# Four tiles of a second MoE moved into the first MoE's last block, and 22 of its 24 tiles transposed by VectorE and DMA

## Chip, cores, metric

One core of a Trainium2 chip. The metric is device time in microseconds (us), median of the runs; the profile is of one execution of the same program.

## What is computed

A linear attention over 4 sequences of 768 steps gives 3072 tokens of 384 features. Two MoE layers follow. Cut to what matters:

```python
# attention, per head: state = w_t * state + k_t v_t^T ;  y_t = r_t (state + u k_t v_t^T)
x = attn_out.transpose(0, 2, 1, 3).reshape(3072, 384)
# first MoE, d_ff = 1536
x = (silu(x @ w_gate) * (x @ w_val)) @ w_out
# second MoE, d_ff = 1024
h = x @ w_in
e = exp(h - max(h))
solu = h * e / (sum(e) + 1e-9)
ln = (solu - mean(solu)) / sqrt(var(solu) + 1e-6) * g_ln
out = ln @ w_out2
```

Every fp32 matrix product is done as three products of a high part and a low part (`xh`, `xl`, and weights split the same way).

## The kernel before

**Planner.** Nothing is issued in program order. Each step is put into a `Graph` with an engine, an assumed duration, a priority (a due time in us), and the keys that it reads and writes. `emit` (line 134) runs a list schedule over these numbers, and the order that comes out is the order on each engine's queue. Each queue then runs in order, so an instruction that waits holds everything behind it. All DMAs are issued from SyncE (SP).

**First MoE.** Tokens come in six blocks of 512 (`q` = 0 to 5). `moe1_unit` (line 744) does one of the 12 slices of `d_ff`: two projections of 9 matmuls of 128x512 into a PSUM bank each (`proj`, gate and value), SiLU on ScalarE (ACT, line 768), the product on VectorE (DVE, line 773), its split into `mh` on ACT and `ml` on DVE (line 776), then 9 matmuls with `w_out` into banks 3 to 5 (`o_part`). At a block's end three copies move the result to SBUF and three DMAs spill it to DRAM (`x2d`). The attention of block q+1 runs inside block q; the last block has none.

**Second MoE.** 24 tiles of 128 tokens, `tile2` (line 982). Weights are staged by DMA (line 922), decoded on DVE and split (lines 934 to 949), and the spilled tokens are loaded again and split (`load_x2`, line 897). A tile is:

- "H": 18 matmuls of 128x512 into `hp`, two PSUM banks (line 998);
- row maximum on DVE (line 1011), exponential on ACT (line 1013), product with `hp` on DVE (line 1016), statistics on DVE in operations of one column (lines 1019 to 1048), normalization on DVE or ACT (`norm`, line 1050);
- transposition of the 128x1024 result. For 8 tiles TensorE (PE) does it in 8 matmuls against the identity (line 1069), and ACT and DVE split the PSUM result into `th` and `tl`. For the 16 tiles in `PAIRS` DVE transposes 32x32 blocks (line 1085), 16 DMAs for each pair of tiles move the blocks across partitions (line 1092), ACT makes `th` and GpSimd (POOL) `tl` (line 977);
- "O": 24 matmuls of 128x384 (line 1104), a copy on ACT, a DMA to the output.

**Memory.** Pools are released and opened again between the stages by steps without an engine (`CTL`): `to_w2` after the attention, `to_p2` and `to_ps2` after all work of the first MoE. So before the change tile 0 alone can start early (`H0`, line 987, `hw`, line 990); every other tile waits for the second half of `hp` or the buffers of `p2`.

Of the kernel before, what the change touches and what calls it, by code (L numbers as in the profile page):

```python
# [30 lines left out]
NQ = S // (2 * C)  # L31
# [7 lines left out]
NEX = 4  # L39
# [12 lines left out]
H0 = -17.0  # L52
TLD = 0
NORM = {"ACT": 1.15, "DVE": 0.73}
GB, NTH = 2, 4
PAIRS = (5, 8, 10, 12, 14, 16, 18, 20)
# [177 lines left out]
def attn_moe_moe2_kernel(  # L234
# [41 lines left out]
    BK = slots(psp, "ps", [128, 512], 6) + slots(psa, "psa", [128, 512], 2)  # L276
# [17 lines left out]
    WD = {d: [w1p.tile([128, 2, KD, 128], F32R, name=f"{x}{d[0][0]}{d[0][1]}") for x in "hl"] for d in duos}  # L294
# [442 lines left out]
    nmid, nsg, silu, spills = [0], [0], [], []  # L737
# [6 lines left out]
    def moe1_unit(j, m):  # L744
# [41 lines left out]
        def later():  # L786
            for k in range(KD):
                o_part(k)
            if m == M1 - 1:
                for k in range(KD):  # L790
                    late = q < NQ - 1
                    if late:
                        xs, xk = ST[k].bitcast(F32), [("st", k, 0), ("st", k, 1)]
                    else:
                        xs, xk = sg_slot() if q == 0 or k < 2 else (None, "x2s0")
                        xk = [xk]

                    def spill(k=k, xs=xs):
# [3 lines left out]
                              [("bank", 3 + k)], xk)  # L802
# [27 lines left out]

    st0, st1 = att_prep(0), att_prep(1)
# [22 lines left out]
    last_unit, R = pend, {}  # L854

    def release(name):
        pools.pop(name)[0].close()

    def to_w2():
        release("st1")  # L860
        release("att")
        release("psa")
        R["h"] = [open_pool("ps2a", space=PSUM, side="right", reuse_waits="tile").tile([128, F2], F32, name="hp0")]
        p = open_pool("w2", side="right", reuse_waits="tile")
        R["i2h"], R["i2l"] = (p.tile([128, KD, F2], F32R, name=x) for x in ("i2h", "i2l"))
        R["o2h"], R["o2l"] = (p.tile([128, M2, DM], F32R, name=x) for x in ("o2h", "o2l"))
        R["g"] = p.tile([128, M2], F32, name="g_sb")
        raw, n = p.tile([128, 2 * F2], RAW, name="sv"), max(DM * sz, TB)
        R["st"] = [raw[:, i * n:(i + 1) * n] for i in range(2)]
        R["ex"] = [raw[:, 0:F2].bitcast(F32)]  # L870
        R["dc"] = slots(p, "dv", [128, DM], 2, U32)
        R["x2s0"] = p.tile([128, TB], F32, name="x2s0")
        R["sm"] = slots(p, "sm", [128, 16], NEX)
        R["bs"] = slots(p, "bs", [128, 2, 6], NEX)

    def to_ps2():
        release("ps")
        p = open_pool("ps2", space=PSUM, reuse_waits="tile")
        R["h"].append(p.tile([128, F2], F32, name="hp1"))
        R["b"] = slots(p, "pb", [128, 512], 4)  # L880

    def to_p2():
        release("w1")
        p = open_pool("p2", reuse_waits="tile")
        R["x2s"] = slots(p, "x2s", [128, TB], 3)
        R["ex"] += slots(p, "ex", [128, F2], NEX - 1)
        R["th"] = slots(p, "th", [128, M2, 128], NTH, F32R)
        R["tl"] = slots(p, "tl", [128, M2, 128], NTH, F32R)
        R["tb"] = slots(p, "tb", [128, GB, F2], 2)
        R["xt"] = slots(p, "xt", [128, GB, 4, F2 // 4], 2)  # L890
        R["ob"] = slots(p, "ob", [128, DM], 3)
# [3 lines left out]
    g.add("CTL", 0.0, 0.0, to_w2, [], ["w2"], after=st_nodes)  # L895
    g.dma(0.1, T5, lambda: nc.sync.dma_start(out=R["g"], in_=g_ln), ["w2"], ["g"])
    def load_x2(q, prio):
        for k in range(KD):
            xk = "x2s0" if q == 0 else ("x2s", k)

            def x2s(k=k):
                return R["x2s0"] if q == 0 else R["x2s"][k]

            g.dma(0.8, prio, lambda k=k, v=x2s: nc.sync.dma_start(out=v(), in_=x2d[q][:, k]),
                  [("x2d", q, k), "w2" if q == 0 else "p2"], [xk])
            g.add("ACT", t_act(TB), prio, lambda k=k, v=x2s: copy(XH[q % 2][:, k], v())(),
                  [xk], [("xh", q % 2, b) for b in range(B)] + [("x2h", q % 2, k)])
            g.alt({"DVE": t_dve(TB)} if q == 0 else {"POOL": t_pool(TB)}, prio,
                  lambda e, k=k, v=x2s: tt(ENG[e], XL[q % 2][:, k], v(), XH[q % 2][:, k].bitcast(F32), ALU.subtract)(),
                  [xk, ("x2h", q % 2, k)], [("xl", q % 2, b) for b in range(B)] + [("x2l", q % 2, k)], port=True)  # L910

    pieces = [("i", k, c0, cn) for k in range(KD) for c0, cn in ((0, 384), (384, 384), (768, 256))]
    pieces += [("o", m, 0, DM) for m in range(M2)]
    for j, (w, k, c0, cn) in enumerate(pieces):
        pr = T5 + 2.0 * j
        i = j % 2
        if j == XP:
            load_x2(0, pr)
        sk, dk = ("sv", i), ("dv", i)
# [8 lines left out]
        def step(z, i=i, cn=cn, raw=raw):  # L928
            decode_op(z, R["st"][i][:, 0:2 * cn].rearrange("p (n t) -> p n t", t=2), raw())
# [32 lines left out]
    shuffled, late = [n + j for n in PAIRS for j in range(GB)], []  # L962

    def splits2(n, s2, j, pt):
        j3 = n % NTH
        xk = [("xt", s2, a, p) for a in range(4) for p in range(4)]

        def ops(y, hi):
            v = slice(4 * y, 4 * y + 4)
            x = R["xt"][s2][:, j].rearrange("p a (m t) -> p m a t", m=M2)[:, v]  # L970
            h, l = (R[z][j3][:, v].rearrange("p m (a t) -> p m a t", a=4) for z in ("th", "tl"))
            if hi:
                copy(h, x)()
            else:
                return l, x, h.bitcast(F32)

        for y in range(2):
            g.add("ACT", t_act(512), pt + SPL, partial(ops, y, True), xk, [("th", j3, y)])
            g.alt({"POOL": t_pool(512), **({"DVE": t_dve(512)} if TLD else {})}, pt + SPL,
                  lambda e, y=y: tt(ENG[e], *ops(y, False), ALU.subtract)(), xk + [("th", j3, y)], [("tl", j3, y)])  # L980

    def tile2(n):
        q, b = order[n]
        i = n % NEX
        j3 = n % NTH
        jb = n % 3
        p0 = TEND + 8.0 * n + (0 if n else H0)
        s = slice(b * 128, (b + 1) * 128)
        hk = [("hb", n % 2, 0), ("hb", n % 2, 1)]
        hw = "ps2" if n % 2 else "w2"  # L990
        xh_, xl_ = XH[q % 2], XL[q % 2]

        def hp():
            return R["h"][n % 2]

        def h_mm(j):
            f = slice(j * 512, (j + 1) * 512)
# [5 lines left out]
        for j in range(2):  # L1003
            g.add("PE", 2.06, p0 + 2 * j, lambda j=j: h_mm(j),
                  [(x, q % 2, k) for x in ("x2h", "x2l") for k in range(KD)] + i2keys + [hw], [hk[j]])

        def c(x):
            return R["sm"][i][:, x:x + 1]

        pr = p0 + -12.0  # L1010
        g.add("DVE", 1.15, pr, lambda: DVE.tensor_reduce(out=c(0), in_=hp(), axis=AX.X, op=ALU.max, negate=True),
              hk, [("m", i)])
        g.add("ACT", 1.1, pr, lambda: ACT.activation(out=R["ex"][i], in_=hp(), func=AF.Exp, bias=c(0), scale=1.0,
                                                     accum_out=c(2)), hk + [("m", i), "table", "p2" if i else "w2"],
              [("ex", i), ("s", i)] + [("sv", z) for z in range(0 if n else 2)])
# [12 lines left out]
        def ts2(out, in0, s1, s2, op0, op1=None):
            kw = {} if op1 is None else {"op1": op1}
            return lambda: DVE.tensor_scalar(out=c(out), in0=c(in0), scalar1=s1, scalar2=s2, op0=op0, **kw)  # L1030

        def mul3(out, x, y, z):
            return lambda: DVE.scalar_tensor_tensor(out=c(out), in0=c(x), scalar=-1.0 if z == 11 else c(y),
                                                    in1=c(y if z == 11 else z), op0=ALU.mult, op1=ALU.mult)
# [61 lines left out]
        def finish():  # L1096
            if n in shuffled:
                splits2(n, s2, j2, pt)
# [114 lines left out]
```

## Time and profile before

| | us |
|---|---|
| median of 3 runs (755.42 to 755.64) | 755.6 |
| the profiled execution | 756.6 |
| its span in the trace | 754.8 |
| PE busy in the span | 744.7 |
| DVE busy | 568.0 |
| ACT busy | 327.5 |
| POOL busy | 60.7 |

The profiled execution took 1.0 us more than the median, and 1.8 us of it lie outside the span. Matmuls are pipelined, so a row's duration overlaps the next one; what a matmul takes from PE is the distance from its start to the next start. The stages in the trace: attention and first MoE to about 550 us, second MoE from there to the end, with the last block of the first MoE from about 476 us.

### The profile page before, as it was taken

To read this page: it belongs to the slowest core of one execution; us is meant where nothing else is said; L and a number is where in the kernel's file an instruction comes from. 1 tells how busy PE (TensorE), PEld (TensorE's weight loads), DVE (VectorE), ACT (ScalarE), POOL (GpSimd) and SP (SyncE) were. 2 spreads that over 40 slices of the span, in tenths; PEclk is the share of its full clock that TensorE was granted. 3 is DMA by queue.
4 is the path that set the end of the run, shared out by engine and by line. 5 is a ranking of instruction groups with operands and counts; after the bars stand their busy time and mean duration, and the time that the engine had idled before them with its cause. 6 is when DMAs were issued, how large, how long until landed. Compare 5 with 4: busy or idle time off the path is not lost.

```text
span 754.8 us, 16325 instructions
## 1 busy us (share of the span) xinstructions
PE 744.7 (99%) x6512; PEld 647.3 (86%) x6512; DVE 568.0 (75%) x1188; ACT 327.5 (43%) x700; POOL 60.7 (8%) x53
## 2 busy tenths in 40 slices
PE   7999999999999999999999999999999999999998
PEld 7899988899888888888888888888788988889998
DVE  8799999978867777767865552588388899999930
ACT  4898653533334333323433312434245352554531
POOL 0000000000000000000000000000022231622440
PEclk9999999999999999999999999999999999999999
DMA  8986643432423223333332210543041224234321
GB/s 232 283 257 236 187 123 110 122 92 82 127 63 101 80 78 114 105 88 89 95 103 75 61 30 10 164 136 120 0 137 53 67 63 126 73 101 107 100 85 43
DMA packets 58780, 81.52 MB, mean 108 GB/s; under 512 B 18128, under 2 KB 42448, under 8 KB 58704
## 3 DMA queue, kind: packets, MB, share of 16 engines
q1 hardware_dynamic: 58704, 80.48, 36.6%
q8 instruction: 51, 0.84, 0.5%
q14 instruction: 25, 0.20, 0.1%
HBM read 59.47 MB, written 9.44 MB: 91 GB/s over the span
## 4 chain that ended last, share of the span: by engine, by line
PE 80%; DVE 10%; DMA 4%; ACT 3%; issue 2%; SPq 1%; ACTq 0%; DVEq 0%
PE ps L733 14%; PE ps L734 14%; PE ps L735 14%; PE pb L1107 4%; PE pb L1109 4%; PE pb L1108 4%; PE hp L999 4%; PE hp L1000 4%; PE hp L1001 4%; PE psa L733 3%; PE psa L734 3%; PE psa L735 3%; DMA feat<-feat 2%; SPq L1092 1%; PE ps L661 1%
## 5 line engine op out<-in xcount | busy, mean ns | idle before, releaser
L733 PE MATMUL ps<-xh,hg 128*128 128x512 f32 (+1 forms) x339 | 124.2, 366 | 0.0
L735 PE MATMUL ps<-xh,lg 128*128 128x512 f32 (+1 forms) x339 | 122.5, 361 | 0.0
L734 PE MATMUL ps<-xl,hg 128*128 128x512 f32 (+1 forms) x339 | 122.4, 361 | 0.0
L733 PE MATMUL ps<-mh,ho 128*128 128x512 f32 (+1 forms) x252 | 91.5, 363 | 0.0
L734 PE MATMUL ps<-ml,ho 128*128 128x512 f32 (+1 forms) x252 | 90.6, 360 | 0.1
L325 ACT ACTIVATE mh<-sg 128x512 fp32r<-128x512 f32 (+1 forms) x84 | 47.7, 570 | 99.0 <-DVE sg L322 98.5
L735 PE MATMUL ps<-mh,lo 128*128 128x512 f32 (+1 forms) x252 | 90.4, 359 | 0.0
L733 PEld LDWEIGHTS ps<-xh,hg 128*128 128x128 f32 x339 | 64.0, 189 | 10.0
L735 PEld LDWEIGHTS ps<-xh,lg 128*128 128x128 f32 x339 | 64.0, 189 | 10.0
L734 PEld LDWEIGHTS ps<-xl,hg 128*128 128x128 f32 x339 | 64.0, 189 | 9.4
L322 DVE TENSOR_TENSOR sg<-sg,ps 128x512 f32<-128x512 f32 (+1 forms) x62 | 37.1, 599 | 44.4 <-PE ps L735 43.3
L322 DVE TENSOR_TENSOR ml<-sg,mh 128x512 fp32r<-128x512 f32 (+1 forms) x84 | 51.0, 608 | 22.2 <-ACT mh L325 21.9
L322 POOL TENSOR_TENSOR xl<-x2s,xh 128x512 fp32r<-128x512 f32 x15 | 19.6, 1328 | 589.3 <-ACT xh L325 589.3
L1107 PE MATMUL pb<-o2h,th 128*128 128x384 f32 x192 | 64.9, 338 | 0.6 <-ACT ob L325 0.6
L1109 PE MATMUL pb<-o2h,tl 128*128 128x384 f32 x192 | 64.5, 336 | 0.0
L1108 PE MATMUL pb<-o2l,th 128*128 128x384 f32 x192 | 64.5, 336 | 0.0
L768 ACT ACTIVATE sg<-ps 128x512 f32<-128x512 f32 (+1 forms) x51 | 28.0, 549 | 78.2 <-PE ps L735 77.9
L733 PE MATMUL psa<-xh,hg 128*128 128x512 f32 (+1 forms) x165 | 60.1, 364 | 0.0
L735 PE MATMUL psa<-xh,lg 128*128 128x512 f32 (+1 forms) x165 | 58.6, 355 | 0.0
L734 PE MATMUL psa<-xl,hg 128*128 128x512 f32 (+1 forms) x165 | 58.6, 355 | 0.0
L999 PE MATMUL hp<-i2h,xh 128*128 128x512 f32 x144 | 57.0, 396 | 0.5 <-DVE sv L1016 0.5
L1000 PE MATMUL hp<-i2l,xh 128*128 128x512 f32 x144 | 56.6, 393 | 0.0
(173 smaller groups left out, 1679.7 us busy)
## 6 DMA issues: line engine op xcount, KB each, us to landing
tok<-tok SPq DMA_DIRECT2D x20, 576.0 KB, 3.8
feat<-feat SPq DMA_DIRECT2D x24, 448.0 KB, 4.5
xt<-tb SPq DMA_DIRECT2D x128, 64.0 KB, 2.0
feat<-feat SPq DMA_DIRECT2D x24, 231.4 KB, 2.7
vv<-vv SPq DMA_DIRECT2D x24, 192.0 KB, 2.7
st<-w_gate SPq DMA_DIRECT2D x12, 384.0 KB, 4.7
st<-w_val SPq DMA_DIRECT2D x12, 384.0 KB, 5.9
st<-w_out SPq DMA_DIRECT2D x12, 384.0 KB, 5.1
```

Of the source, the lines that this page charges most:

```text
L322: return lambda: eng.tensor_tensor(out=out, in0=in0, in1=in1, op=op)
L325: return lambda: ACT.activation(out=out, in_=in_, func=AF.Copy)
L733: PE.matmul(out=o, lhsT=wh, rhs=xhi, start=first, stop=False, **kw)
L734: PE.matmul(out=o, lhsT=wh, rhs=xlo, start=False, stop=False, **kw)
L735: PE.matmul(out=o, lhsT=wl, rhs=xhi, start=False, stop=last, **kw)
L768: lambda: ACT.activation(out=sg, in_=pg.t[:, 0:n], func=AF.Silu), [pg.key], [sk]))
L999: PE.matmul(out=hp()[:, f], lhsT=xh_[:, k, s], rhs=R["i2h"][:, k, f], start=(k == 0), stop=False)
L1000: PE.matmul(out=hp()[:, f], lhsT=xh_[:, k, s], rhs=R["i2l"][:, k, f], start=False, stop=False)
L1001: PE.matmul(out=hp()[:, f], lhsT=xl_[:, k, s], rhs=R["i2h"][:, k, f], start=False, stop=(k == KD - 1))
L1107: PE.matmul(out=po(), lhsT=th[:, m], rhs=R["o2h"][:, m], start=(m == 0), stop=False)
L1108: PE.matmul(out=po(), lhsT=th[:, m], rhs=R["o2l"][:, m], start=False, stop=False)
L1109: PE.matmul(out=po(), lhsT=tl[:, m], rhs=R["o2h"][:, m], start=False, stop=(m == M2 - 1))
```

## The change

- Tiles 0 to 3 of the second MoE may start inside the first MoE's last block: they need `w2` alone (one `hp`, `H0` = -56), and their exponentials are put between two loads of ScalarE's function tables (`early`), since that block's SiLU needs another table. There are 12 table loads in place of 2.
- Tiles go in pairs, but for 22 and 23. Maximum, exponential, product and moments stay one tile's (`front`); the rest of the statistics is done for both tiles at once in operations of two columns (`stats`, `back`).
- All pairs, so tiles 0 to 21, are transposed by DVE and DMA (`shuffle`); tiles 22 and 23 by PE (`by_pe`).
- `norm` runs on ACT only.
- PSUM and SBUF are cut into more pools, so that a buffer of the second MoE waits only for what lay in its own place (`to_p2(z)`, `to_psg`, `to_pso`); seven buffers `ex` in place of four; five staging places for `w_in`, lying in the `ex` buffers.
- The attention of the last tiles is spread over a shorter time (`MARG` = 16), and block 4's result is spilled through other buffers.

```diff
-NEX = 4
+NEX = 7
-H0 = -17.0
+H0 = -56.0
+PE2 = -9.0
-NORM = {"ACT": 1.15, "DVE": 0.73}
+NORM = {"ACT": 1.24}
-PAIRS = (5, 8, 10, 12, 14, 16, 18, 20)
+NE = 4
+SOLO, NSM = (22, 23), 4
...
-    ADV, ADV2, MARG = 4.0, 12.0, 0.0
+    ADV, ADV2, MARG = 4.0, 12.0, 16.0
...
-        d = (bstart[j + 1] - bstart[j] - (0.0 if n < NYS else MARG)) / (a1 - a0)
+        d = (bstart[j + 1] - bstart[j] - (MARG if n >= NT - B else 0.0)) / (a1 - a0)
...
+    SV = [(2,), (4,), (3,), (0, 1)]
...
-        i = j % 2
+        i, y = j % 2, (0, 1, 4, 3, 2)[j % 5] if w == "i" else j % 2
...
-    g.add("CTL", 0.0, 0.0, to_p2, [], ["p2"], after=[i for i in work if i not in spills])
-    g.add("CTL", 0.0, 0.0, to_ps2, [], ["ps2"], after=work)
+    for z in range(M1 // 2):
+        g.add("CTL", 0.0, 0.0, partial(to_p2, z), ["w2"] + ([("p2", z - 1)] if z else []),
+              [("p2", z)] + [(x, y, m) for x in ("wh", "wl") for y in "gvo" for m in (2 * z, 2 * z + 1)])
+    g.add("CTL", 0.0, 0.0, to_psg, ["w2"], ["psg"], after=gvs)
+    g.add("CTL", 0.0, 0.0, to_pso, ["psg"], ["pso"], after=gvs + spills)
...
+    def tile_p0(n):
+        return TEND + 8.0 * n + (H0 if n < NE else 0)
...
+        def early():
+            ACT.preload_act_table_set("natural_log_exp_and_others")
+            if last is not None:
+                last()
+            soft()
+            ACT.preload_act_table_set("silu_and_others")
...
+    def stats(gi, grp):
...
+        g.add("DVE", 0.25, pr, lambda: two(6, 5, 3)(), kv + [("is", z)], [("v0", z)], port=True)
+        g.add("DVE", 0.25, pr, lambda: two(6, 6, 3)(), [("is", z)], [("v0", z)], port=True)
...
+        def log():
+            ACT.activation(out=c(7), in_=c(6), func=AF.Ln)
+            ACT.activation(out=c(7), in_=c(7), func=AF.Exp, scale=-0.5)
...
+    def back(gi, grp):
...
+            g.alt(NORM, pr, norm, [("nb", z), ("rs", z)], [("ex", i)], port=True)
+        (shuffle if w == GB else by_pe)(gi, grp)
...
+    def shuffle(gi, grp):
+        s2, pt = pairs.index(grp) % 2, tile_p0(grp[-1]) + 10.0
+        for j, n in enumerate(grp):
+            g.add("DVE", 1.24, pt - 22.0, lambda j=j, n=n: DVE.transpose(
...
+        for a in range(4):
+            for p in range(4):
+                g.dma(0.66, pt - 9, lambda a=a, p=p: nc.sync.dma_start(
...
+                g.add("POOL", t_pool(512), pt + SPL, lambda y=y, f=ops: tt(POOL, *f(y, False), ALU.subtract)(),
...
+        g.add("PE", 4.17, TEND + 8.0 * n + 35.0 + (LAG if lag else 0), o_mm,
```

How the instructions move, at three places. **PE, tile 1's way to its O, just behind the first MoE** (`hp` is H's result, `ident,ex` a transposition, `pb` and `pc` O's result). Before:

```order
L1001 MATMUL hp_5949<-i2h,xl_97 128x512
L1069 MATMUL pb_5950<-ident,ex_5926 128x128 x4
L1069 MATMUL pb_5951<-ident,ex_5926 128x128 x4
L999 MATMUL hp_5400<-i2h,xh_96 128x512
L1000 MATMUL hp_5400<-i2l,xh_96 128x512
L1001 MATMUL hp_5400<-i2h,xl_98 128x512
```

After:

```order
L1016 MATMUL hp_6092<-i2h,xh_117 128x512
L1017 MATMUL hp_6092<-i2l,xh_117 128x512
L1018 MATMUL hp_6092<-i2h,xl_119 128x512
L1185 MATMUL pc_6178<-o2h,th_5977 128x384
L1186 MATMUL pc_6178<-o2l,th_5977 128x384
L1187 MATMUL pc_6178<-o2h,tl_6047 128x384
```

The 8 transpositions of the tile are gone; over the whole program PE has 64 before and 16 after, and 48 instructions fewer in all (4964 and 4916), nothing else on PE being added or taken away.

**ACT in the first MoE's last block** (`sg` is the SiLU, `mh` the split of the product, `o2h` the weights of the second MoE, `ex` with `sm` the exponential of a tile). Before, the end of the block:

```order
L768 ACTIVATE sg_100<-ps_80 128x512
L936 ACTIVATE o2h<-dv_5410,g_sb 128x384
L325 ACTIVATE mh_102<-sg_100 128x512
L768 ACTIVATE sg_99<-ps_79 128x512
L325 ACTIVATE mh_101<-sg_99 128x512
L768 ACTIVATE sg_100<-ps_78 128x512
L960 ACT_TABLE_LOAD
L1013 ACTIVATE sv,sm_5413<-hp_5400,sm_5413 128x1024
L325 ACTIVATE mh_102<-sg_100 128x512
```

After, from the block's third slice on:

```order
L329 ACTIVATE mh_122<-sg_120 128x512
L960 ACTIVATE o2h<-dv_5302,g_sb 128x384
L960 ACTIVATE o2h<-dv_5301,g_sb 128x384
L1035 ACT_TABLE_LOAD
L1032 ACTIVATE ex_5298,sm_5304<-hp_5288,sm_5304 128x1024
L1039 ACT_TABLE_LOAD
L772 ACTIVATE sg_121<-ps_100 128x512
L960 ACTIVATE o2h<-dv_5302,g_sb 128x384
L960 ACTIVATE o2h<-dv_5301,g_sb 128x384
L329 ACTIVATE mh_123<-sg_121 128x512
```

Each early tile's exponential stands between two table loads, ahead of the SiLU of a later slice.

**SP, the loads of the second MoE's weights and tokens** (`sv` and `ex` are staging places, `w_in` and `w_out` here the second MoE's weights, `x2d` the spilled tokens). Before:

```order
L922 DMA sv<-w_in 128x768 x2
L904 DMA x2s_5412<-x2d_89 128x512
L922 DMA sv<-w_in 128x512
L922 DMA sv<-w_in 128x768
L904 DMA x2s_5412<-x2d_89 128x512
```

After:

```order
L946 DMA ex_5300<-w_in 128x512
L927 DMA ex_5298<-x2d_110 128x512
L946 DMA sv<-w_out 128x768 x2
L927 DMA ex_5299<-x2d_110 128x512
L332 DMA x2d_114<-sg_121 128x512
L332 DMA x2d_114<-x2s_5303 128x512
L332 DMA x2d_114<-sg_120 128x512
L946 DMA sv<-w_out 128x768 x2
L927 DMA x2s_5303<-x2d_110 128x512
```

The last third of the first 512 tokens is loaded into the buffer through which block 4's last third was just spilled, behind two more weight loads.

## Rows read from the trace of the kernel before

**Rows 1.** The page's first part: busy time and instructions of each engine.
```profile
PE 744.7 (99%) x6512; PEld 647.3 (86%) x6512; DVE 568.0 (75%) x1188; ACT 327.5 (43%) x700; POOL 60.7 (8%) x53
```
**Rows 2.** Windows: stretch, its length, busy time by engine, granted clock, DMA share.
```profile
375.00:450.00 75.00, 75.00 (x698) 61.98 (x697) 44.26 (x89) 24.87 (x53) 0.00 (x0) 1.00 0.23 68
505.00:535.00 30.00, 30.00 (x133) 24.70 (x133) 22.62 (x43) 10.08 (x18) 0.00 (x0) 1.00 0.32 93
535.00:555.00 20.00, 19.50 (x90) 15.85 (x89) 9.40 (x20) 8.65 (x15) 0.00 (x0) 1.00 0.20 67
635.00:720.00 85.00, 85.00 (x431) 77.15 (x430) 80.16 (x171) 43.67 (x90) 34.22 (x27) 1.00 0.38 99
```
**Rows 3.** Chain that ended last, at the first MoE's end: start, length, what.
```profile
542.57 1.28 ACT L960
...
543.86 1.21 ACT sv L1013 x2
...
545.25 1.14 DVE sv L1016
...
546.44 0.50 PE hp L999
```
**Rows 4.** Timeline of PE at its two waits: start, length, instruction, idle time before.
```profile
545.55 0.39 PE L735 MATMUL ps<-mh,lo 128*128 128x512 f32 x1
546.44 0.50 PE L999 MATMUL hp<-i2h,xh 128*128 128x512 f32 x1 [0.50 <-DVE sv L1016]
...
626.12 0.39 PE L1001 MATMUL hp<-i2h,xl 128*128 128x512 f32 x1
627.06 0.45 PE L1107 MATMUL pb<-o2h,th 128*128 128x384 f32 x1 [0.56 <-ACT ob L325]
```
**Rows 5.** Timeline of PE at one tile's transposition.
```profile
568.11 1.03 PE L1069 MATMUL pb<-ident,ex 128*128 128x128 f32 x8
568.90 0.48 PE L999 MATMUL hp<-i2h,xh 128*128 128x512 f32 x1
```
**Rows 6.** Groups by line: count, busy us, mean ns of one, idle before and releaser.
```profile
L322 DVE TENSOR_TENSOR ml<-sg,mh 128x512 fp32r<-128x512 f32 (+1 forms) x84 | 51.0, 608 | 22.2 <-ACT mh L325 21.9
L325 ACT ACTIVATE mh<-sg 128x512 fp32r<-128x512 f32 (+1 forms) x84 | 47.7, 570 | 99.0 <-DVE sg L322 98.5
L322 POOL TENSOR_TENSOR tl<-xt,th 128x512 fp32r<-128x512 f32 x32 | 40.6, 1298 | 81.7 <-ACT th L325 73.6 <-DMA out<-ob 8.1
L322 DVE TENSOR_TENSOR sg<-sg,ps 128x512 f32<-128x512 f32 (+1 forms) x62 | 37.1, 599 | 44.4 <-PE ps L735 43.3 <-ACT sg L768 0.7
...
L1011 DVE TENSOR_REDUCE sm<-hp 128x1 f32<-128x1024 f32 x24 | 29.2, 1216 | 6.0 <-PE hp L1001 5.5
L768 ACT ACTIVATE sg<-ps 128x512 f32<-128x512 f32 (+1 forms) x51 | 28.0, 549 | 78.2 <-PE ps L735 77.9
```
**Rows 7.** Chain, a pair of tiles shuffled: product of the second, first DMA issue, landing.
```profile
597.25 1.13 DVE ex L1016
...
602.11 0.68 SPq L1092
...
611.80 2.00 DMA xt<-tb
```
**Rows 8.** One line's and one tile's instructions: count, ns min/median/max, first and last start.
```profile
L922 SPq DMA_DIRECT2D sv<-w_in x9: 328/328/447, 476.2 to 499.9; - x9
...
L322 DVE TENSOR_TENSOR i2l<-dv,i2h x9: 416/551/559, 483.7 to 505.9; 128x384 fp32r<-128x384 f32 x6, 128x256 fp32r<-128x256 f32 x3
```
**Rows 9.** Timeline of DVE, the last attention tile: sum of its output, split of it.
```profile
449.73 0.62 DVE L322 TENSOR_TENSOR tok<-psa,tok 128x192 f32<-128x192 f32 x2 [0.98 <-PE psa L664]
...
463.62 0.56 DVE L322 TENSOR_TENSOR xl<-tok,xh 128x384 fp32r<-128x384 f32 x1 [1.33 <-ACT xh L325]
```
**Rows 10.** DMA issues: count, KB each, median us from issue to landing.
```profile
x2s<-x2d SPq DMA_DIRECT2D x18, 256.0 KB, 2.8
...
x2d<-st SPq DMA_DIRECT2D x15, 256.0 KB, 2.8
```

More of the change, by code (lines that the diff above doesn't have):

```diff
@@ L801, in later @@
                     x = g.add("ACT", t_act(n), p0 - 20, lambda k=k, v=spill: copy(v(), bank(3 + k)[:, 0:n])(),
-                              [("bank", 3 + k)], xk)
+                              [("bank", 3 + k)] + ([] if late else ["w2"]), xk)
                     if j == len(blocks) - 1:
@@ L853, in attn_moe_moe2_kernel @@
                 st_nodes.extend(range(first, len(g.opts)))
[L854 to L891, printed above, removed]
+    last_unit = pend
     T5 = bstart[-1]
     w1_nodes = list(range(len(g.opts)))
-    g.add("CTL", 0.0, 0.0, to_w2, [], ["w2"], after=st_nodes)
     g.dma(0.1, T5, lambda: nc.sync.dma_start(out=R["g"], in_=g_ln), ["w2"], ["g"])
@@ L983, in tile2, with hkeys, front @@
+    groups, n = [], 0
+    while n < NT:
+        groups.append((n,) if n in SOLO else (n, n + 1))
+        n += len(groups[-1])
+    pairs = [x for x in groups if len(x) == GB]
+    def hkeys(n):
+        return [("hb", max(0, n - NE) % 2, j) for j in range(2)]
+    def tile_p0(n):
+        return TEND + 8.0 * n + (H0 if n < NE else 0)
+    def front(n, gi, j, last):
         q, b = order[n]
[L984 to L987, printed above, removed]
+        i, z = n % NEX, gi % NSM
+        p0 = tile_p0(n)
@@ L1007, in c @@
         def c(x):
[L1008 to L1015, printed above, removed]
@@ L1028, in ts2 @@
[L1028 to L1034, printed above, removed]
-        small_op(ts2(2, 2, EPS_SUM, None, ALU.add), ["s"], ["s1"])
@@ L1116, in tile2 @@
-        if n in shuffled:
-            late.append(finish)
-            if j2 == GB - 1:
-                while late:
-                    late.pop(0)()
-        else:
-            finish()
-    for n in range(NT):
-        if n % B == 0 and n // B + 1 < NQ:
-            load_x2(n // B + 1, TEND + 8.0 * n + X2)
-        tile2(n)
+            return R["sm"][z][:, x, j:j + 1]
+        pr = p0 + (PE2 if n < NE else -12.0)
+        g.add("DVE", 1.2, pr, lambda: DVE.tensor_reduce(out=c(0), in_=hp(), axis=AX.X, op=ALU.max, negate=True),
+              hk + ["w2"], [("m", z, j)])
@@ new lines, in front @@
+        if n < NE:
+            g.add("ACT", 4.2 + (0 if last is None else 0.4), pr, early, exr + ([] if last is None else [("v", gi % NSM - 1)]),
+                  exw + ([] if last is None else [("ln", gi % NSM - 1)]))
+        else:
+            g.add("ACT", 1.3, pr, soft, exr + ["table"], exw)
+        g.add("DVE", 1.2, pr, lambda: DVE.tensor_tensor(out=R["ex"][i], in0=R["ex"][i], in1=hp(), op=ALU.mult),
+              hk, [("ex", i)])
+        for y in range(2):
+            g.add("DVE", 0.68, pr, lambda y=y: DVE.bn_stats(out=R["bs"][z][:, j, y], in_=R["ex"][i][:, y * 512:(y + 1) * 512]),
+                  [("ex", i)], [("bs", z, j, y)])
@@ new lines, in alone @@
+    def alone(log):
+        ACT.preload_act_table_set("natural_log_exp_and_others")
+        log()
+        ACT.preload_act_table_set("silu_and_others")
+    last = None
+    for gi, grp in enumerate(groups):
+        for j, n in enumerate(grp):
+            if n % B == 0 and n // B + 1 < NQ:
+                load_x2(n // B + 1, TEND + 8.0 * n + X2)
+            mine = last if n < NE else None
+            front(n, gi, j, mine)
+            if mine is not None:
+                back(gi - 1, groups[gi - 1])
+                last = None
+        log = stats(gi, grp)
+        if grp[-1] + 1 < NE:
+            last = log
+        elif grp[-1] < NE:
+            g.add("ACT", 3.0, tile_p0(n) + PE2 - 5.0, partial(alone, log), [("v", gi % NSM)], [("ln", gi % NSM)])
+            back(gi, grp)
+        else:
+            g.add("ACT", 0.4, tile_p0(n) - 17.0, log, [("v", gi % NSM), "table"], [("ln", gi % NSM)])
+            back(gi, grp)
@@ L1128, in fill @@
+    for n in pairs[-1]:
+        finish(n, True)
     def fill(i):
```

286 lines of the change are left out of this document (175 added, 111 removed).

## Prediction, made before the changed kernel was run

> **What bounds the kernel now.** I read the page's first part, then windows over the stages, then the chain and PE's timeline where a window is not full. PE is busy for 744.7 of 754.8 us [rows 1]. Busy time alone proves little, because matmuls overlap, so look at windows inside the part that the change touches: from 505 to 535 us PE is busy for 30.00 of 30.00 us at a granted clock of 1.00, and 133 matmuls start in them, one every 0.226 us; from 635 to 720 us for 85.00 of 85.00 [rows 2]. There 431 matmuls start. A tile of the second MoE has 18 (H) and 24 (O), so 431 are 10.3 tiles of 8.3 us; 18 x 0.226 = 4.1 of them are H and 4.2 are O. PE is the bound, and the time changes by what PE no longer does or no longer waits for.
>
> The window from 535 to 555 us is not full (19.50 of 20.00). The chain of waits shows why: a load of ScalarE's function table of 1.28 us, an exponential of 1.21, a product of 1.14, and only then the H matmul [rows 3]. On PE's timeline that matmul starts 0.89 us after its predecessor, 0.66 more than the usual 0.23. There is one more such place: at 627.06 an O waits for an ACT copy that frees its bank: 0.94 us from start to start, 0.71 too many [rows 4].
>
> DVE is at 80.16 of 85.00 us in the steady stage and has hardly room; ACT is at 43.67 and POOL at 34.22 [rows 2].
>
> **The change, part by part.**
>
> *PE transpositions.* The order has 64 before and 16 after, so six tiles of eight lose theirs. The eight matmuls start at 568.11 and the next matmul at 568.90; that one lasts 0.48 in place of 0.39 [rows 4, 5]. That is 0.79 + 0.09 = 0.88 us a tile and 6 x 0.88 = **5.3 us**, all on the path, since PE is full around it. Nothing else is added to PE.
>
> *The two waits.* The first is tile 0's: its exponential now comes tens of microseconds before the block's end. The second came from an ACT queue held by exponentials waiting for DVE. Bounds: nothing, if the new order puts waits of this size elsewhere, and 0.66 + 0.71 = **1.4 us**. I take 1.4 and charge new waits separately.
>
> *New waits.* The trace cannot show them. Bounds: nothing, since PE ran 85 us without one in a planned order [rows 2], and several us, worked out below. I take **0.3 us**, half of one like the two seen.
>
> *H of tile 0, moved into the first MoE's last block.* It is the largest risk. In the new order 231 matmuls stand between the last attention matmul and this H: 231 x 0.226 = 52 us. If `w_in` is late, all of PE waits. Now: from the sum of the last attention tile's output (449.73) to the end of its split (464.2) pass 14.5 us [rows 9], and from the first `w_in` load (476.2) to the end of the last low part (506.5) 30.3 us [rows 8], with two staging places and DVE also serving the block. One after the other that is 45 us, so 7 us are left, and more with five places. The tokens are tighter. Their last third goes through the buffer from which block 4's last third is spilled. From that block's last matmul to H stand 51 matmuls, 11.5 us. In them lie a copy (0.57), a store and a load (2.8 each, [rows 10]), a copy and a subtraction (0.57 and 0.61, as in [rows 6]): 7.4 us. The 4 us left must take in two `w_out2` loads, which stand ahead on SP's queue and wait for staging places that DVE must free.
>
> *Table loads.* Ten more. An early tile holds ACT for two loads, 2 x 1.28, and an exponential, 1.21 [rows 3]: 3.8 us in which a SiLU may wait. The tightest is tile 3. From the end of its H: gate projection 2.0, SiLU 0.55, load, exponential, load, and the split on ACT 0.57, then DVE's queue with a product, moments and the split: done at about 8.2 us [rows 3, 6]. Before that slice's O part PE has six groups of nine matmuls, 12.2 us. 4 us are left, elsewhere 7 or more. So I cost them at nothing; were this cover gone, each would cost up to its 3.8 us. In the trace the exponential starts 0.01 us after the load ends (542.57 + 1.28 and 543.86, [rows 3]). The Trainium skill ("ScalarE: Activation LUTs", What ACT_TABLE_LOAD costs, and its rules) speaks against the change: a switch is to be budgeted at 2.66 us, 1.38 of it a drain, and one set's work finished before the next. The trace has no such drain at its load; by that price the 4 us shrink to 1.2, and the sum would stay the same, but with a greater chance of the table rival.
>
> *The shuffle of all pairs.* SP issues 16 DMAs from 602.11 to 611.80, 9.7 us for a pair [rows 7], while PE spends 2 x 8.3 = 16.6 us on it: SP keeps up, with outputs and reloads in the remaining 7 us. Latency: the maximum 1.22 [rows 6], an exponential 1.21 [rows 3], 16.6 from the product to the landing [rows 7], a copy 0.57 and two POOL subtractions of 1.30 [rows 6], and some 2.4 for the pair's second normalization and transposition: 25 us. The first pair that does not come early is tiles 4 and 5; in the new order 6 H and 3 O stand between tile 5's H and tile 4's O, 37 us. 12 us hide what DVE's and ACT's queues put in between.
>
> *DVE, ACT, POOL.* DVE loses normalization, half of the small operations and the `tl` of six tiles, and gains their transposition, so its 94% falls. ACT gains normalization, about 18 operations of the exponential's size over the whole stage, and has 41 us free in 85 [rows 2]. POOL gains twelve subtractions, 16 us, and loses three of the reload's; it is at 40%. All of this lies beside PE.
>
> *Attention of the last tiles in a shorter time, and the tail.* Up to block 4 the order is the same on every engine. The attention that is drawn together lies in the window from 375 to 450 us, where PE is full and DVE busy for 44.26 of 75.00 us [rows 2]. Drawn together by 16 us in all, DVE would come to about 44 of 59, still less than in the steady stage. The end is unchanged: last O, copy, DMA. Nothing.
>
> **Sum.** 5.3 + 1.4 - 0.3 = 6.4 us less. The span goes from 754.8 to 748.4, the profiled execution from 756.6 to 750.2. The median lies 1.0 below that execution, so 755.6 - 6.4 = **749.2 us**.
>
> **Rivals.**
>
> 1. *Waits in the new order, of 1 to 4 us together*: H of tile 0 a little late behind its tokens, or an O behind an ACT queue. For: only 4 us of cover at that place, on an SP queue with waiting loads in front. Against: the planner's durations for matmuls, exponential and shuffles agree with the rows, and only two waits were left before. Time: 750.2 to 753.2.
> 2. *Table switches hold PE.* Were a switch 1.4 us dearer than the row has it, or ACT's queue otherwise 4 us late, the O part after each of the five switches would wait about 1 us: 755.6 - 6.7 + 5 = 754, no change. Against: the row has no gap behind the load. This is the outcome that the skill's rule on grouping by table set points to.
> 3. *The other side: `w_in` or the tokens reach H of tile 0 far too late.* H stands in order, so PE waits for the whole of it, and everything behind moves. It decides from 7 + 6.7 + 1.5, some 15 us, later than the rows say for the weights, or 12 for the tokens. It would take loads that cannot start until the attention's buffers are free, and DVE, full from decoding, serving the block's products first. With 19 us the time is 755.6 - 6.7 + 12 = 761. Against: the 30 us of [rows 8] already hold this competition.
> 4. *The change's saving is not there*, because the pairs' shuffles are late in the steady stage and PE waits where it transposed. It needs 12 us more latency than the sum above, and then costs each pair; the same time as in 2 or 3.
>
> **Chances.** Forecast within 748.2 and 750.2: 0.66. Rival 1: 0.21. Rivals 2 and 4 near 754: 0.05. Rival 3 and 4 on the far side: 0.04. Below 748.2, if first matmuls behind a wait (0.1 each) and others go too: 0.04. A measurement of this kernel can tell about 0.2% from no change, 1.5 us. Faster by more, below 754.1: 0.92; within: 0.04; slower: 0.04. The range 748.0 to 752.5 holds the forecast and most of rival 1.
>
> **What would show it.** Right: 16 transpositions on PE; PE full in windows from 480 us to the end, with no gap over 0.3 us; H of tile 0 with no idle time before it; the span's last matmul some 6 us earlier. Wrong: idle time on PE before the first `hp` matmuls released by the token split on DVE or by its DMA (rivals 1, 3); before an O part released by `ml` after a table load (2); before an O released by `tl` on POOL (4). If PE is full and the time has not fallen by 5 us, the price of a transposition is wrong.

## The result, and the profile after

The changed kernel takes **749.01 us** (median of 4 runs, 748.27 to 749.97) beside 755.51 of the kernel before (4 runs): ratio 0.9917, 95% interval 0.9900 to 0.9934. The forecast was 749.2. The profiled execution took 749.21 us, its span 747.4.

The page's first part, which answers to [rows 1]:

```profile
PE 739.1 (99%) x6464; PEld 643.6 (86%) x6464; DVE 550.3 (74%) x1105; ACT 356.1 (48%) x706; POOL 71.6 (10%) x62
```

And the windows of [rows 2], with the same columns:

```profile
375.00:450.00 75.00, 75.00 (x698) 61.98 (x697) 45.39 (x90) 24.61 (x51) 0.00 (x0) 1.00 0.27 77
505.00:535.00 30.00, 30.00 (x133) 24.66 (x132) 17.56 (x35) 15.54 (x20) 0.00 (x0) 1.00 0.22 60
535.00:555.00 20.00, 20.00 (x90) 16.57 (x89) 7.93 (x18) 12.39 (x18) 3.45 (x3) 1.00 0.12 27
635.00:720.00 85.00, 85.00 (x443) 78.46 (x442) 67.33 (x133) 46.97 (x84) 34.22 (x27) 1.00 0.39 97
```

PE has 48 matmuls less. The window that was not full is full; in the steady one 443 matmuls start in place of 431, and DVE has come down from 80.16 to 67.33 us. The view of PE's waits (what waited, for what: us, times, longest) has no row from the second MoE any more:

```profile
PE ps L1222 <- DMA ident<-eye: 3.8, 1, 3.8
PE psa L715 <- DVE tok L326: 0.5, 1, 0.5
PE psa L516 <- ACT sg L772: 0.4, 1, 0.4
```

All three lie in the first 144 us. That PE is now the chain shows in part 4 of the page: PE had 80% of the chain, and has 93%.

Spans differ by 7.4 us, more than the medians. Part of it lies ahead of the change: one attention matmul at the start of block 2 (number 2800 of PE's order, counted from 0, in every kernel here) starts at 228.11 us before and at 227.19 after. So all kernels below are also compared from this matmul to PE's last one. PE's timeline at both ends, before:

```profile
228.11 0.22 PE L664 MATMUL ps<-RO,feat 48*64 48x48 f32 x2
...
751.03 0.34 PE L1109 MATMUL pb<-o2h,tl 128*128 128x384 f32 x1
```

and after:

```profile
227.19 0.22 PE L668 MATMUL ps<-RO,feat 48*64 48x48 f32 x2
...
743.70 0.34 PE L1187 MATMUL pc<-o2h,tl 128*128 128x384 f32 x1
```

522.92 and 516.51 us: **6.41 us less** in the part that the change touches; the sum of the prediction was 6.4. Of this stretch, the times from start to start add up to 6.33 us for 64 transpositions before and 1.58 for 16 after (4.75 less), to 100.22 and 98.98 for H (1.24 less), 293.59 and 293.03 for the first MoE's matmuls (0.56 less), 100.13 and 100.27 for O (0.14 more).

### The profile page after: what moved, and what is told of

Same layout as the page of the kernel before. It is cut to its first block, busy times and chain, and to the rows that moved or that the text cites. A ratio compares the mean times of both kernels' runs of the same rounds, so it can differ in the third digit from the quotient of the medians.

```text
span 747.4 us, 16227 instructions
## 1 busy us (share of the span) xinstructions
PE 739.1 (99%) x6464; PEld 643.6 (86%) x6464; DVE 550.3 (74%) x1105; ACT 356.1 (48%) x706; POOL 71.6 (10%) x62
## 4 chain that ended last, share of the span: by engine, by line
PE 93%; DVE 3%; DMA 2%; ACT 1%; issue 0%; SPq 0%; ACTq 0%; DVEq 0%
PE ps L737 15%; PE ps L738 15%; PE ps L739 15%; PE hp L1016 4%; PE hp L1017 4%; PE hp L1018 4%; PE psa L737 4%; PE psa L738 4%; PE psa L739 4%; PE pc L1187 2%; PE pb L1187 2%; PE pb L1185 2%; PE pc L1185 2%; PE pb L1186 2%; PE pc L1186 2%; PE ps L1222 2%
## 5 line engine op out<-in xcount | busy, mean ns | idle before, releaser
L326 POOL TENSOR_TENSOR tl<-xt,th 128x512 fp32r<-128x512 f32 x44 | 55.8, 1296 | 643.4 <-DVE ml L326 550.5
L1018 PE MATMUL hp<-i2h,xl 128*128 128x512 f32 x144 | 56.0, 389 | 0.0
L738 PEld LDWEIGHTS ps<-ml,ho 128*128 128x128 f32 x252 | 47.6, 189 | 7.4 <-DVE ml L326 0.5
L737 PEld LDWEIGHTS ps<-mh,ho 128*128 128x128 f32 x252 | 47.6, 189 | 7.4 <-ACT mh L329 0.3
```

The source lines that it names most:

```text
L326: return lambda: eng.tensor_tensor(out=out, in0=in0, in1=in1, op=op)
L737: PE.matmul(out=o, lhsT=wh, rhs=xhi, start=first, stop=False, **kw)
L738: PE.matmul(out=o, lhsT=wh, rhs=xlo, start=False, stop=False, **kw)
L1018: PE.matmul(out=hp()[:, f], lhsT=xl_[:, k, s], rhs=R["i2h"][:, k, f], start=False, stop=(k == KD - 1))
```

## The experiments

All are edits of the changed kernel. Times are medians; the kernel before had 755.29, 755.39 and 755.27 us in the three groups (runs 1 to 4, 5 to 8, 9 to 12).

**1. Eight tiles transposed by PE again.** Here O of tiles 14 and 15 stands behind the eight last tiles and multiplies what these left in the `th` and `tl` places, so these two results are not the right ones; the amount of work is unchanged.

```diff
-SOLO, NSM = (22, 23), 4
+SOLO, NSM = tuple(range(16, 24)), 4
```

> Tiles 16 to 23 are transposed by TensorE, 8 tiles as before the change, all else as in the changed kernel (749.0 us). Theory (TensorE is full from 80 us to the end, and a tile's transposition costs it 0.88 us): six more tiles cost 6 x 0.88 = 5.3 us, 754.3 us, and the window from 560 to 720 us stays full on TensorE. Rival (the gain came from the two removed waits and from a lighter VectorE, not from the transpositions themselves): under 751 us.

754.18 us (753.37 to 756.05), ratio 0.9991 [0.9981, 1.0000]. From the shared matmul to the last pass 521.76 us, 5.25 more than the changed kernel for six tiles: 0.875 a tile, the priced 0.88. DVE keeps its room here (59.24 of 80 us from 640 to 720), so the gain is PE's own time, not DVE's relief.

**2. No tile transposed by PE.**

```diff
-SOLO, NSM = (22, 23), 4
+SOLO, NSM = (), 4
```

> No tile is transposed by TensorE; tiles 22 and 23 go by DMA too. Theory: TensorE loses 2 x 0.88 = 1.8 us, but the last pair's way of some 26 us from its H to its O lies beside only six O of 4.2 us, 25 us, so TensorE waits 0.5 to 2 us before the last two O: 747.7 to 749.2 us. Rival (the shuffles of the last pair are held up by the output DMAs and by POOL): a wait of over 4 us and over 751 us.

754.32 us (753.06 to 755.89), ratio 0.9991 [0.9981, 1.0002]: the theory missed, nearly the whole gain is gone. PE's waits in this kernel:

```profile
PE pb L1185 <- ACT th L329: 2.8, 2, 2.3
PE pb L1187 <- POOL tl L326: 1.5, 2, 0.7
```

Its chain of waits from 715 us to the end, as shares of that stretch:

```profile
by line: SPq L1155 42.5%; issue 6.4%; SPq L1192 5.5%; DMA xt<-tb 5.5%; PE pc L1187 4.9%; PE pc L1186 4.8%; PE pb L1187 4.6%; PE pc L1185 4.3%; POOL tl L326 3.6%; PE pb L1186 3.4%; PE pb L1185 3.3%; ACT ob L329 2.7%; POOLq L326 0.5%; ACTq L3
```

The chain at the end runs through SP's issues (L1155). While H and O alternate, PE spends 16.6 us on a pair; behind the last H only 8.3, and a pair's 16 issues, one every 0.64 us, take 10.2. PE's timeline at the first two waits:

```profile
723.80 0.34 PE L1187 MATMUL pc<-o2h,tl 128*128 128x384 f32 x1
726.46 0.44 PE L1185 MATMUL pb<-o2h,th 128*128 128x384 f32 x1 [2.32 <-ACT th L329]
726.73 0.34 PE L1186 MATMUL pb<-o2l,th 128*128 128x384 f32 x1
727.81 0.69 PE L1187 MATMUL pb<-o2h,tl 128*128 128x384 f32 x1 [0.74 <-POOL tl L326]
728.29 0.52 PE L1185 MATMUL pb<-o2h,th 128*128 128x384 f32 x1
728.61 0.52 PE L1186 MATMUL pb<-o2l,th 128*128 128x384 f32 x1
```

Four matmuls of the last two pairs wait and start 2.49, 0.90, 0.68 and 0.91 us late: 5.0 us. Behind the first two waits, from 728.29 on, ten matmuls start mostly 0.32 us apart in place of 0.17, at the lower of the two granted levels (1.2 GHz; from 723.8 to 731.2 us the granted clock has a mean of 0.77): 1.6 us more. With 0.3 us right behind the waits that is 6.9 us, against 1.8 saved: 521.66 us between the two matmuls, 5.15 more than the changed kernel. The two tiles that the change leaves to PE are what fills this time; the prediction did not see this part of theirs.

**3. No early tiles.**

```diff
-NE = 4
+NE = 0
```

> No tile of the second MoE runs inside the first MoE's last block; the table is loaded once, after the last SiLU. Theory (the four early tiles are what hides the shuffle's latency of 25 us at the start of the second MoE): TensorE must cover it with H alone, VectorE needs some 5 us for a tile's part where H takes 4.1, and TensorE waits 5 to 12 us in the first 40 us of the second MoE: 754 to 761 us. Rival (seven exponential buffers and banks released one by one are enough): no wait over 1 us and under 750.5 us.

757.09 us (756.30 to 759.17), ratio 1.0032 [1.0013, 1.0052]. PE's waits in this kernel:

```profile
PE hp L1016 <- DVE ex L1048: 3.3, 2, 2.8
PE hp L1016 <- DVE sv L1048: 3.0, 1, 3.0
```

PE's timeline at one of them (start, length, instruction, idle time before):

```profile
563.87 0.40 PE L1018 MATMUL hp<-i2h,xl 128*128 128x512 f32 x1
567.26 0.52 PE L1016 MATMUL hp<-i2h,xh 128*128 128x512 f32 x1 [3.00 <-DVE sv L1048]
567.60 0.61 PE L1017 MATMUL hp<-i2l,xh 128*128 128x512 f32 x1
568.01 0.63 PE L1018 MATMUL hp<-i2h,xl 128*128 128x512 f32 x1
568.44 0.63 PE L1016 MATMUL hp<-i2h,xh 128*128 128x512 f32 x1
```

All tiles start after the first MoE, DVE has the maxima, products and moments of several at once, and H waits for a bank. The waits come to 6.8 us. Eight and seven matmuls behind the two long ones start 0.43 us apart in place of 0.23, at the lower of the two granted levels (1.2 GHz; from 560 to 580 us the granted clock has a mean of 0.91): most of the 3.3 us that are left of the 10.1 by which this execution exceeds the changed kernel between the two matmuls (526.57). It was the slowest of its five.

**4. Banks handed over together.** The PSUM banks of the second MoE wait for all work of the first, as before the change.

```diff
-    g.add("CTL", 0.0, 0.0, to_psg, ["w2"], ["psg"], after=gvs)
-    g.add("CTL", 0.0, 0.0, to_pso, ["psg"], ["pso"], after=gvs + spills)
+    g.add("CTL", 0.0, 0.0, to_psg, ["w2"], ["psg"], after=work)
+    g.add("CTL", 0.0, 0.0, to_pso, ["psg"], ["pso"], after=work)
```

> The PSUM banks for the second half of H and for O are given over only when all work of the first MoE is done, as before the change, so the first O no longer stands ahead of the last slice's O part. Theory: that slice's product and split take 1.8 us (0.60, 0.57, 0.61) behind its value projection, and TensorE has 2.0 us of the slice before to do; the reloaded tokens of the next block need about 4 us against 4.1: a wait of 0 to 1 us, 749.0 to 750.0 us. Rival (the first O in that place is what keeps TensorE full there): a wait of 2 to 4 us, 751 to 753 us.

749.78 us (748.73 to 750.13), ratio 0.9930 [0.9915, 0.9945]; between the two matmuls 516.98, 0.47 more: the matmul at 557.87 starts 0.31 us late behind a wait, and the one behind it 0.11. The separate banks carry half a microsecond at most.

**5 and 6. More table loads behind each early exponential**, two and six of them (`range(1)` and `range(3)`):

```diff
             soft()
+            for _ in range(1):
+                ACT.preload_act_table_set("silu_and_others")
+                ACT.preload_act_table_set("natural_log_exp_and_others")
             ACT.preload_act_table_set("silu_and_others")
```

> Two more table loads are issued behind each of the four early exponentials' first load (2 x 1.28 = 2.57 us more of ScalarE per early tile, 10.3 us in all); TensorE's order stays as it is. Theory (loads lie beside PE): in the trace of the changed kernel the low part of a SiLU's product that follows an early exponential is ready 5.2, 6.2, 6.5 and 3.7 us before the out part that reads it starts (tiles 0 to 3), so 2.57 us more fit everywhere: 748.5 to 749.6 us, no new wait on PE. Rival (a switch of tables costs PE something that the rows of ScalarE don't show, such as a drain): each added load then adds its part to the time, 0.5 us or more each: 753 us or more.

749.02 us (748.47 to 749.71), ratio 0.9918 [0.9903, 0.9932]. ACT is busy for 54.62 us from 480 to 560 in place of 45.10, and between the two matmuls pass the same 516.51 us.

> Six more loads behind each early exponential's first (6 x 1.28 = 7.7 us per early tile); TensorE's order stays. Theory: 7.7 us exceed all four covers (5.2, 6.2, 6.5, 3.7 us), so PE waits 2.5, 1.5, 1.2 and 4.0 us before the out part behind each early tile, some 9 us in all, less where a wait earlier gives cover to the next: 754 to 759 us, the longest wait at tile 3. Rival (SiLU's place on ScalarE's queue isn't what holds PE; products come from earlier slices): below 751 us.

761.50 us (761.23 to 762.13), ratio 1.0081 [1.0064, 1.0098]. ACT's timeline at tile 0:

```profile
492.13 1.12 ACT L1032 ACTIVATE ex<-hp,sm 128x1024 f32<-128x1024 f32 x1
493.15 0.19 ACT L1032 ACTIVATION_READ_ACCUMULATOR ex<-hp,sm 128x1 f32 x1
493.36 1.28 ACT L1040 ACT_TABLE_LOAD   x1
494.65 1.28 ACT L1041 ACT_TABLE_LOAD   x1
```

PE's longest wait in the same kernel:

```profile
PE ps L737 <- ACT mh L329: 6.7, 2, 3.8
```

The sign is as expected, and so is the longest wait, at tile 3 (3.97 us late; 4.0 expected). At tiles 0 to 2 PE is late by 0.6 (a gate projection, for its bank, and not an out part), 3.0 and 0.1 us, where 2.5, 1.5 and 1.2 were expected. The three waits come to 7.6 us, not 9; the time is above the range expected, since the matmuls behind the two longer waits start 0.43 us apart, as in 3: 12.5 us in all between the two matmuls. So loads lie beside PE up to the cover, and what exceeds it costs PE more than itself.

**7. Attention of the last tiles not drawn together.**

```diff
-    ADV, ADV2, MARG = 4.0, 12.0, 16.0
+    ADV, ADV2, MARG = 4.0, 12.0, 0.0
```

> The attention of the last eight tiles is no longer drawn together (its margin of 16 us set to 0); the early tiles stay early. In the new order 180 matmuls stand between the last attention matmul and the first H, in place of 231: 11.5 us less for the weights. Theory: the last w_in part was ready some 10 us before H needed it, so the margin is used up and H waits 0 to 1.5 us: 749.0 to 750.5 us. Rival 1 (drawing together costs PE or DVE something): under 748.3 us. Rival 2 (weights far later, since their staging places wait for the attention's buffers): H waits 3 us or more, over 752 us.

749.04 us (748.08 to 749.66), ratio 0.9916 [0.9901, 0.9931]; 516.69 between the two matmuls. The last split of `w_in` comes 16 us later than in the changed kernel (489.94 and 473.96), 0.3 us after H of tile 0 has started, which the planner has put 21 matmuls further on. The timeline of this kernel:

```profile
489.65 0.40 PE L1016 MATMUL hp<-i2h,xh 128*128 128x512 f32 x1
...
489.94 0.43 DVE L326 TENSOR_TENSOR i2l<-dv,i2h 128x256 fp32r<-128x256 f32 x1
```

Its columns are read by H's last matmul but one alone, 16 x 0.23 = 3.7 us behind its first. No wait: drawing the attention together bought cover that nothing needs. (`MARG` acts on the last four tiles, `n >= NT - B`, not on eight, as the expectation has it.)

**8 and 10. No tile transposed by PE, the last two pairs issued on two queues.** This is run 2 with half of these pairs' issues on ACT's queue.

```diff
-SOLO, NSM = (22, 23), 4
+SOLO, NSM = (), 4
...
+                two = gi >= len(pairs) - 2 and a % 2
-                g.dma(0.66, pt - 9, lambda a=a, p=p: nc.sync.dma_start(
+                g.add("DMA2" if two else "DMA", 0.66, pt - 9, lambda a=a, p=p, two=two: (nc.scalar if two else nc.sync).dma_start(
```

> All 24 tiles shuffled as in the run without transpositions, but of the last two pairs every second group of shuffles is issued on ScalarE's queue in place of SP's. Theory: behind the last H a pair has only 2 x 4.2 = 8.3 us of PE work, while its 16 issues take 10 us of SP; PE waited 5.3 us at the last four O's for that reason. With two queues the waits fall below 1 us and PE keeps the 1.76 us of two transpositions that it no longer has: 747.2 to 748.6 us. Rival (latency of the last pair, from its moments to POOL's subtraction, holds PE, not the issue): waits of 3 us or more stay, 750.5 to 754 us.

748.22 us, but 746.90 to 752.35; ratio 0.9916 [0.9886, 0.9946]. So it was run again beside the changed kernel itself:

> The changed kernel as it is, beside the runs of this group: 749.0 us, as before, and the scale for the next run.

> The same kernel as the one with two queues at the end, in more rounds, beside the changed kernel, since its four times lay far apart (746.9 to 752.4 us). Theory: 1.8 us less than the changed kernel in the same group, as between the 2800th matmul and the last one (514.70 us here, 516.51 there): 746.9 to 747.8 us, with a few runs that have a wait somewhere. Rival: the times scatter because this kernel's end hangs on the two queues, and the median is no better than the changed kernel's (over 748.5 us).

The changed kernel: 748.78 us (747.71 to 749.30), ratio 0.9911 [0.9897, 0.9924]. With two queues: **747.70 us** (746.36 to 747.89), ratio 0.9895 [0.9881, 0.9908]. The intervals overlap, but between the two matmuls it is 514.70 us in both of its profiled executions and 516.51 in both of the changed kernel's, 1.81 less, two transpositions (1.76) and no wait. The execution of 752.35 us in run 8 was not profiled; what held it is open. PE's timeline of the last run:

```profile
227.53 0.22 PE L668 MATMUL ps<-RO,feat 48*64 48x48 f32 x2
...
742.23 0.34 PE L1188 MATMUL pc<-o2h,tl 128*128 128x384 f32 x1
```

The wait of run 2 was SP's issue time, and not the transfers. The Trainium skill ("DMA: Bandwidth & Descriptors", Issuing engines are not separate DMA queues) says that issuing from several engines saves only the sequencer's issue time, usually small beside the transfer. The first half agrees; here the issues are not small: 0.64 us each, 16 in a row, 10.2 us beside 2.0 to a landing.

**11. Statistics tile by tile.** Each small operation of a pair is issued once per column:

```diff
+        cur = [0]
...
+        def each(fn):
+            def run():
+                for cur[0] in range(w):
+                    fn()
+            return run
...
-            return R["sm"][z][:, x, 0:w]
+            return R["sm"][z][:, x, cur[0]:cur[0] + 1]
...
-            g.add("DVE", 0.25, pr - 5, fn, [(x, z) for x in reads] + kv, [(writes, z)], port=True)
+            g.add("DVE", 0.25, pr - 5, each(fn), [(x, z) for x in reads] + kv, [(writes, z)], port=True)
```

> The small operations of a pair's statistics are issued once per tile on a single column in place of once per pair on two (ten more on VectorE per pair, and two on ScalarE); the order of TensorE stays. Theory (they lie beside PE): VectorE, 79% busy in the steady stage, rises by some 10 x 0.12 to 0.2 us in 16.6 us, to about 88%, ScalarE by 0.4 us: no change, 748.5 to 749.8 us. Rival (statistics by pairs carry part of the gain, through VectorE's queue): 750.5 us or more, with waits of PE before H on VectorE.

749.75 us (749.17 to 750.43), ratio 0.9925 [0.9911, 0.9938], with 516.55 us between the two matmuls (516.51): pairs or not, PE does the same. The 1.0 us by which this median lies above its neighbour's is not in that part, and the intervals overlap. DVE rose less than expected, from 62.91 to 65.51 of 80 us (640 to 720).

**12. Half of the shuffle's transfers issued twice**, unknown to the planner.

```diff
-                g.dma(0.66, pt - 9, lambda a=a, p=p: nc.sync.dma_start(
-                    out=R["xt"][s2][32 * p:32 * p + 32, :, a],
-                    in_=R["tb"][s2][32 * a:32 * a + 32, :, 256 * p:256 * p + 256]),
+                g.dma(0.66, pt - 9, lambda a=a, p=p: [nc.sync.dma_start(
+                    out=R["xt"][s2][32 * p:32 * p + 32, :, b],
+                    in_=R["tb"][s2][32 * b:32 * b + 32, :, 256 * p:256 * p + 256])
+                    for b in ((a,) if a < 2 else (a, a - 2))],
```

> Of each pair's 16 shuffle transfers eight are issued a second time (same data to the same place): 24 issues per pair, 15.4 us of SP in place of 10.2, unknown to the planner; the order of TensorE stays. Theory (SP keeps up, latency has 12 us of cover): each pair's data comes 5 us later, and with two outputs SP is then busy 16.5 of 16.6 us a pair; no wait in the steady stage. At the end the pair of tiles 20 and 21 is ready 4.5 us before its first O in the changed kernel, and now 5 to 10 us later: a wait of 0.5 to 5.5 us: 749.5 to 754.5 us. Rival (no such cover: O's in the steady stage wait for POOL's subtraction): waits of 3 us or more before 700 us, over 757 us.

776.05 us (774.09 to 777.44), ratio 1.0272 [1.0254, 1.0289]: the rival, and my theory failed. The chain from 560 us to the end:

```profile
by line: SPq L1155 48.5%; DMA xt<-tb 6.9%; ACT th L329 6.1%; issue 5.0%; ACT ex L1032 2.6%; ACT ex L1109 2.6%; PE pb L1186 2.2%; PE pb L1187 2.1%; PE pb L1188 2.1%; PE pc L1188 2.1%; SPq L1193 2.0%; PE pc L1186 1.9%; PE pc L1187 1.9%; DVE b
```

The longest waits of PE, and ACT's for the shuffles:

```profile
PE hp L1016 <- DVE ex L1048: 11.1, 5, 6.6
PE pc L1132 <- ACT ex L1109: 6.1, 1, 6.1
...
PE pc L1186 <- ACT ob L329: 2.3, 1, 2.3
...
ACT th L329 <- DMA xt<-tb: 59.7, 10, 9.4
```

The pairs' first issues come 18.6 us apart (589.0 to 738.0 for eight) where PE needs 16.6. I had SP at 16.5 us a pair, with two outputs, but left out the three reloads (1.5 us behind some pairs), and that SP is a queue in order: where an output waits for a late O, as at 627.84 and 665.88, the next pair's issues wait behind it. PE's first wait (before the matmul at 627.81) is an O's for `tl`; then ACT, in order too, stands for 59.7 us at `th` copies whose data has not landed, the exponentials behind them come late, so does DVE's product, and H finds no bank free. 5 us of latency became 27 us of time by going round this loop; some 5 of the 27 are matmuls at the lower granted level behind the waits of 6.6 and 6.1 us.

## Why the prediction was right, point by point

- **Transpositions, 5.3.** 48 take 4.75 us less, and six matmuls behind them no longer start 0.09 late: 5.3. Run 1 gives the same price when it puts them back.
- **Removed waits, 1.4.** Both are gone, with the 0.11 us by which the matmul behind each was late: 1.6. What removed each of them, the early exponential and a freer ACT queue, is the prediction's reading; no run takes the two apart.
- **New waits, 0.3.** There are none. The rest of the sum is of another kind: some 0.5 us in hundreds of tiny differences, 0.4 of it in the 576 O matmuls. Right total, wrong name: 5.3 + 1.6 - 0.5 = 6.4. That the waits brought 0.2 more than priced and the losses took 0.2 more, so that the total fits to a hundredth, is luck.
- **H of tile 0.** No wait, yet the covers were mis-sized both ways. The weights' last split ended 10.5 us before H's start (I had 7), and run 7 shows that it may end after it. The tokens were tighter than my "4 us less two loads", for a reason that I did not price. The third that goes through the spill's buffer lands at 482.01, and it is the first that H reads, so ACT and DVE split it first. The other two had landed by 472.9, but their splits stand behind it in these two queues and end at 484.31 + 1.29 = 485.60, after H's start. No wait comes of it, since H reads them from its sixth and its ninth matmul on (486.02 and 486.71, the weight loads 0.2 us earlier): 0.8 and 0.9 us are left. The timeline of the changed kernel:

```profile
482.03 0.64 ACT L329 ACTIVATE xh<-x2s 128x512 fp32r<-128x512 f32 x1 [2.76 <-DMA x2s<-x2d]
...
484.31 1.29 DVE L326 TENSOR_TENSOR xl<-ex,xh 128x512 fp32r<-128x512 f32 x2
...
484.86 0.40 PE L1016 MATMUL hp<-i2h,xh 128*128 128x512 f32 x1
...
486.71 0.39 PE L1018 MATMUL hp<-i2h,xl 128*128 128x512 f32 x1
```

- **Table loads, nothing.** The low part that follows an early exponential is ready 5.2, 6.2, 6.5 and 3.7 us before its reader (I had 7 and, at tile 3, 4). Runs 5 and 6 bracket it. Rival 2's "about 1 us" at each switch does not follow from its own numbers: two loads 1.4 us dearer leave 1.2 of the 4 us of cover. In run 6's rows a load starts 0.02 us behind the accumulator read (493.15 + 0.19, 493.36) and the next one 0.01 behind the first. The Trainium skill ("ScalarE: Activation LUTs", What ACT_TABLE_LOAD costs) adds a drain of 1.38 us to a load of 1.283: the load agrees, the drain appears at no load here.
- **Shuffle latency, 25 us against 37: the step that was mis-sized.** From the end of tile 5's H (572.0) to tile 4's low part (606.97) pass 35.0 us, and its O starts 2.1 us later. The timeline there:

```profile
571.61 0.40 PE L1018 MATMUL hp<-i2h,xl 128*128 128x512 f32 x1
...
575.43 1.21 DVE L1048 TENSOR_TENSOR ex<-ex,hp 128x1024 f32<-128x1024 f32 x1
...
585.59 2.36 DVE L1149 STREAM_TRANSPOSE tb<-ex 128x1024 f32<-128x1024 f32 x2
...
587.98 1.23 SPq L1155 DMA_DIRECT2D xt<-tb  x2
...
604.41 5.08 POOL L326 TENSOR_TENSOR tl<-xt,th 128x512 fp32r<-128x512 f32 x4 [13.05 <-DMA out<-ob]
...
609.10 0.33 PE L1185 MATMUL pb<-o2h,th 128*128 128x384 f32 x1
```

(Two of the four subtractions are tile 4's: 604.41 + 2.56 = 606.97. They follow ACT's `th` copies, which begin at 603.72, whatever releaser the row names.) Most of the 10 us that the sum missed lies between the product (575.43) and the first issue (587.98): 12.6 us, where [rows 7] have 4.9. In between DVE and ACT serve the maxima and exponentials of the next tiles. I counted 12 us of cover as spare for these queues; they use nearly all of it there, and the other tiles that do not come early have 3 to 19 us left. "SP keeps up" held, but with less to spare than I wrote. In [rows 7] 611.80 is where the last of the 16 issues begins, so a pair takes SP 10.3 us and not 9.7; in the changed kernel 94.3 of the 132 us from 588 to 720 are issues, and run 12 adds 5 us a pair and loses 27 in all.
- **Not foreseen: the end.** "Last O, copy, DMA. Nothing" is true only because the last two tiles go by PE. In the program's order the transpositions and O's of tiles 22 and 23 stand ahead of the last pair's O's. POOL ends tiles 20 and 21 at 730.95, and tile 20's O starts 4.6 us later:

```profile
725.93 5.02 POOL L326 TENSOR_TENSOR tl<-xt,th 128x512 fp32r<-128x512 f32 x4 [9.39 <-ACT th L329]
...
735.55 0.33 PE L1185 MATMUL pb<-o2h,th 128*128 128x384 f32 x1
```

The forecast would have missed by 5 us, had the change shuffled all 24 tiles (run 2).

What stays open: why the time ahead of the shared matmul, where the kernels have the same order, differs by up to 3.1 us between the profiled executions (225.74 us in run 2, 228.80 in run 8); no run was made for it.

## What to carry to other kernels

Where one engine is full, price what leaves it from its own rows: here a tile's transposition came out to a hundredth (0.88 priced, 0.875 in run 1). The risk sits in what used to wait beside it, so list for each moved operation when its data is ready and when its first reader starts. A queue that keeps up in the steady stage can bound the end, where the work that paced it runs out: compare issues per tile with the full engine's work per tile there too. And compare executions from an instruction that all kernels share, since what varies ahead of the change can be as large as a term of the sum.

## What the runs showed of the hardware

- In runs 2, 3 and 6 a wait of PE of 2.5 to 4.0 us cost more than itself: behind it six to eight matmuls of 128x512 started 0.43 us apart in place of 0.23, or nine of 128x384 0.32 in place of 0.17, some 1.6 us on top. Behind two waits in run 12, which made the matmuls at 690.73 and 732.15 start 3.0 and 2.4 us late, it did not happen: the length of the wait alone does not tell.
- Table loads followed each other and an exponential without a visible drain: 1.28 us each, with 0.01 to 0.02 between.
- An issue of a shuffle takes SP 0.59 us, 0.64 from one to the next; on ACT's queue 0.61. With 24 in place of 16 a pair the kernel was 27 us slower, while the transfers landed in 2.0 us as before and the DMA engines' share was 0.43.
